# K and V read in 32 KB packets, each written to two partitions through a shape register

## The chip, the cores and the metric

The kernel runs on one core of a Trainium2 chip. The metric is the device time of one execution in microseconds (us). Where a kernel was timed in several rounds, the median is quoted. Before the change the time is 369.1 us.

The page counts 16 DMA engines for the core. A load is issued by one instruction on the queue of SyncE (SP). Each contiguous piece that a load of K or V reads appears in the trace as one *packet*: 64 loads of 128 pieces each, and 8192 packets of 16 KB. The program's tiles lie over 128 partitions of on-chip memory; the loads from DRAM go there. Of the other engines, PE does the matmuls (PEld loads their weights), DVE the transposes and other vector work, ACT and POOL the rest, as the page lists them.

## The reference, cut to what matters

A decode step of attention is mixed with an MLP by a gate. Attention reads the last 2048 keys of a cache, for 8 batches and 16 K/V heads of 128 elements in bf16. K and V of that window are 2 x 8 x 16 x 2048 x 128 x 2 bytes = 134.2 MB of the 154.6 MB that the kernel moves.

```python
k = jnp.repeat(k_cache[:, :, Sk - W:, :], rep, axis=1)      # W = 2048, Sk = 8192, Dh = 128
v = jnp.repeat(v_cache[:, :, Sk - W:, :], rep, axis=1)
scores = jnp.einsum("bhqd,bhkd->bhqk", q, k) * (Dh ** -0.5)
p = _softmax(scores, axis=-1)
o = jnp.einsum("bhqk,bhkd->bhqd", p, v)
...
return g * a + (1 - g) * b        # a: attention @ wo, b: MLP, g: gate
```

Softmax and the sum over keys do not depend on the order of the keys, provided that K and V are ordered alike.

## The kernel before

K and V come in 64 loads of 2 MB, one for four batches of one head ("quad"), into a ring of nine slots. Each load puts 128 pieces of 16 KB (64 keys) into 128 partitions: piece x (of 32) of batch a (of 4) goes to partition 4x + a. The code in question, with cuts:

```python
def run_dma(nc, e, out, in_, shape=None):
    item = 2
    kw = {}
    if shape is not None:
        pst = shape[0]                       # elements in one partition's row
        walk = shape[1]                      # (step, count), slowest first; the last is one contiguous run
        enc = []
        for step, num in reversed(walk[:-1]):
            parts, rest = divmod(step, pst)
            ...
            enc += [parts * 262144 + rest * item, num]
        enc += [0, 1] * (4 - len(enc) // 2)
        kw = dict(dst_dge_shape=enc, bass_dst_dge_shape=tuple(walk))
    return e.add_instruction(mybir.InstDMACopy(..., queue="qSPDynamicHW", mode="Copy",
        ins=e.lower_ap_dma(in_), outs=e.lower_ap_dma(out), **kw))
...
        def src_of(cache, g, q):
            hkv, b0 = 2 * g + q // 2, 4 * (q % 2)
            return cache[b0:b0 + 4, hkv, S0:Sk, :].rearrange("a (x r) d -> x a (r d)", x=32)
...
            # k_unit; v_unit likewise
            d = dma("sp", lambda e: e.dma_start(slot(s), src_of(A_k_cache, g, q)), ...)
            # two DVE transposes of the slot, then QK matmuls from the transposed halves
...
            # wo_chunk: the one load that already goes through the shape register
            src = bass.AP(A_wo.tensor, offset=128 * h0 * D, ap=[[4 * D, 32], [128 * D, WO_CH], [1, 4 * D]])
            d = dma("sp", lambda e: run_dma(nc, e, dst[:, :, 0:D], src, (AST, ((4 * AST, 32), (WOP, WO_CH), (AST, 4), (1, D)))), ...)
```

`AST` is one partition's row, so `(4 * AST, 32)` means "32 times, four partitions further each time". I shall write such a walk as (4 partitions, 32), slowest step first, and leave out the contiguous run at its end. The shape register is the field `dst_dge_shape`. In the program's intent the destination is gone through in that order, while the source is read in the order of its own pattern.

Of the kernel before, what the change touches and what calls it, by code (L numbers as in the profile page):

```python
# [38 lines left out]
class _Plan:  # L39
# [16 lines left out]
    def dma(self, eng, fn, semkey, nbytes, deps=(), name=None, after=(), prio=0):  # L56
        op = _Op(eng, fn, deps, name, self.DMA_ISSUE, after=after, is_dma=True, dma_sem=semkey, nbytes=nbytes, prio=prio)
        op.idx = len(self.all)
        self.all.append(op)
        return op  # L60
# [119 lines left out]
# [4 lines that stand above are left out]
        pst = shape[0]  # L184
        walk = shape[1]
# [3 lines that stand above are left out]
            assert parts == 0 or rest == 0  # L189
# [3 lines that stand above are left out]
    return e.add_instruction(mybir.InstDMACopy(  # L193
        name=nc.get_next_instruction_name(), engine=e.engine, queue="qSPDynamicHW", mode="Copy",
        ins=e.lower_ap_dma(in_), outs=e.lower_ap_dma(out), **kw))


def build_kernel(nc, A_x, A_k_cache, A_v_cache, A_wq, A_wo, B_x, B_w1, B_b1, B_w2, B_b2, gate_w, out):
    B, Sq, D = A_x.shape
    _, Hkv, Sk, Dh = A_k_cache.shape  # L200
    Hq = A_wq.shape[1] // Dh
    F = B_w1.shape[1]
    W = min(4096, max(256, Sk // 4))
# [19 lines left out]
    with ExitStack() as es:  # L223
# [67 lines left out]
        def aoffs(name):  # L291
            return R[name][0] // 2
# [50 lines left out]
        def slot(s):  # L343
            return RAW[:, s * SE:(s + 1) * SE]
# [245 lines left out]
        proj_ops = {}  # L590
        oT_done = {}

        def src_of(cache, g, q):
            hkv, b0 = 2 * g + q // 2, 4 * (q % 2)
            return cache[b0:b0 + 4, hkv, S0:Sk, :].rearrange("a (x r) d -> x a (r d)", x=32)

        def take_slot():
            n = n_slot[0]
# [43 lines left out]
        def k_unit(i):  # L642
            g, q = divmod(i, 4)
            s = take_slot()
            d = dma("sp", lambda e: e.dma_start(slot(s), src_of(A_k_cache, g, q)), "s%d" % s, 4 * W * Dh * 2, deps=slot_free[s], name="dk%d" % i, after=last_dma[-1:])
            last_dma.append(d)
            ub = q
            qrs = []
            for a in range(4):
                def fn(e, a=a):  # L650
                    dst = bass.AP(arena, offset=32 * a * AST + aoffs("qbd") + ub * 512 + 32 * a + 8 * q, ap=[[AST, 32], [128, 4], [1, 8]])
                    src = bass.AP(arena, offset=32 * a * AST + aoffs("q4") + 32 * g + 8 * q, ap=[[AST, 32], [256, 4], [1, 8]])
                    return e.tensor_copy(dst, src)  # L653
                qrs.append(add("pool", fn, deps=[o_q4, o_qz] + [qk_unit.get(i - 4)], name="qr%d_%d" % (i, a), cost=0.2))
            trs = []
            for h in range(2):
                n = 2 * i + h
                kb = n % 2
                deps = [d] + ([qk_half[n - 2]] if n >= 2 else [o_y, o_ssq])
                tr = add("dve", (lambda h=h, kb=kb: lambda e: e.transpose(bass.AP(arena_f, offset=foffs("KT") + kb * 2048, ap=[[AST // 2, 128], [1, 2048]]),  # L660
                                                                         bass.AP(arena_f, offset=foffs("RAW") + s * (SE // 2) + 32 * h, ap=[[AST // 2, 128], [64, 64], [1, 32]])))(),
                         deps=deps, name="tr%d_%d" % (i, h), cost=2.3, after=tr_hist[-1:])
                tr_hist.append(tr)
                trs.append(tr)

                def qk_fn(e, h=h, kb=kb):
                    mm = None
                    if q == 0 and h == 0:
                        e.matmul(ps[:, 0, :], maskL, maskR, start=True, stop=False)  # L669
                        for rc in range(1, 4):  # L670
                            held_matmul(nc, e, ps[:, rc, :], maskL, maskR, start=True, stop=False)
                    for ee in range(2):
                        for rc in range(4):
                            rhs = bass.AP(arena, offset=aoffs("KT") + kb * 4096 + rc * 1024 + ee, ap=[[AST, 128], [2, 512]])
                            args = (ps[:, rc, :], qbd[:, ub, 2 * h + ee, :], rhs)
                            last = q == 3 and h == 1 and ee == 1
                            mm = e.matmul(*args, start=False, stop=last) if rc == 0 else held_matmul(nc, e, *args, stop=last)  # L677
                    return mm
                deps = [tr] + qrs
                if q == 0 and h == 0:  # L680
                    deps += exp_done[g - 1] if g else [o_q4, o_mL, o_mR]
                qk = add("pe", qk_fn, deps=deps, name="qk%d_%d" % (i, h), cost=1.95 + (0.9 if q == 0 and h == 0 else 0), after=qk_half[-1:])
                qk_half.append(qk)
            qk_unit[i] = qk
            slot_free[s] = trs
            if q == 3:
                softmax(g)

        def v_unit(i):
            g, q = divmod(i, 4)  # L690
            s = take_slot()
            item = 2 * g + q // 2
            d = dma("sp", lambda e: e.dma_start(slot(s), src_of(A_v_cache, g, q)), "s%d" % s, 4 * W * Dh * 2, deps=slot_free[s], name="dv%d" % i, after=last_dma[-1:])
            last_dma.append(d)

            def pv_fn(e):
                mm = None
                for t in range(16):
                    c = 32 * (t % 4)
                    mm = e.matmul(ps[c:c + 32, BK_OS[i % 2], :], PT[:, g % 2, 512 * q + 32 * t:512 * q + 32 * t + 32], slot(s)[:, 512 * t:512 * t + 512],  # L700
                                  start=(t < 4), stop=(t >= 12), skip_group_check=True, tile_position=(0, c))
                return mm
            deps = [d] + pt_done[g] + ([u_ev[i - 2]] if i >= 2 else [o_qT, o_u])
            prev = add("pe", pv_fn, deps=deps, name="pv%d" % i, cost=1.5, after=pv_hist[-1:])
            pv_hist.append(prev)
            slot_free[s] = [prev]
            if q == 3:
                pv_last[g] = prev
            u_ev[i] = add("act", lambda e: e.activation(out=EV[:, i % 2, :], in_=ps[:, BK_OS[i % 2], :], func=ACTF.Copy),  # L709
                          deps=[prev] + ([u_sum[i - 2]] if i >= 2 else []), name="uev%d" % i, cost=0.8, prio=3)  # L710

            def us_fn(e):
                mm = None
                for r in range(4):
                    mm = e.matmul(ps[:, BK_S, OC + 16 * (item % 2) + 8 * (q % 2):OC + 16 * (item % 2) + 8 * (q % 2) + 8], EV[:, i % 2, 128 * r:128 * r + 128], i32[:, 8 * r:8 * r + 8],  # L715
                                  start=(r == 0), stop=(r == 3), skip_group_check=True)
                return mm
            u_sum[i] = add("pe", us_fn, deps=[u_ev[i]] + o_i32 + b6_r[-2:], after=b6_w[-1:], name="us%d" % i, cost=1.0, prio=3)
            b6_w.append(u_sum[i])
            if q % 2 == 1:  # L720
                hl = q // 2
                prev = u_sum[i]
                osrc = ps[:, BK_S, OC + 16 * (item % 2):OC + 16 * (item % 2) + 16]
                if item < Hkv - 1:
                    ev = add("act", lambda e: e.activation(out=o32[:, item % 2, :], in_=osrc, func=ACTF.Copy), deps=[prev] + ([oT_done[item - 2]] if item >= 2 else []), name="oev%d" % item, cost=0.25, prio=3)  # L725
                    o_item_ev[item] = ev
                    b6_r.append(ev)
                    eng, src_, deps = "pool", o32[:, item % 2, :], [ev, rg_done[g]]
                else:
                    eng, src_, deps = "dve", osrc, [prev, rg_done[g]]  # L730

                def om_fn(e):
                    return e.tensor_tensor(out=oT[:, item, :, :].rearrange("p h b -> p b h"), in0=src_.rearrange("p (b h) -> p b h", h=2),  # L733
                                           in1=rg[:, g % 2, 16 * hl:16 * hl + 16].rearrange("p (b h) -> p b h", h=2), op=ALU.mult)
                oT_done[item] = add(eng, om_fn, deps=deps, name="oT%d" % item, cost=0.25, prio=9)
# [121 lines left out]
```

## Time and profile before

| what | value |
|---|---|
| time | 369.1 us |
| DMA: K and V packets | 8192 of 16 KB, 611 ns most often, 612 in the mean |
| DMA rate, 45 to 330 us | 430 GB/s, all 16 engines busy |
| DVE, PE busy | 57%, 69% of the span |

The page of the kernel before, its parts on DMA (part 2: busy share of the 16 engines in tenths and GB/s in 40 slices; part 3: the queue's share of 16 engines' time) and on the chain of work that ended last:

```profile
span 367.5 us, 4111 instructions
...
DMA  8999999999999999999999999999999999999994
GB/s 345 428 408 428 428 427 433 432 426 432 435 430 432 422 427 430 432 439 431 426 430 428 422 438 427 430 426 428 433 430 430 428 431 426 433 428 432 418 424 191
DMA packets 11851, 154.59 MB, mean 421 GB/s; under 512 B 1292, under 2 KB 1332, under 8 KB 3000
...
q1 hardware_dynamic: 11776, 154.29, 98.6%
...
DMA 74%; DVE 12%; PE 11%; SPq 1%; ACT 1%; issue 1%; DVEq 0%; ACTq 0%
```

All 16 engines are busy from the first slice to the last but one, and three quarters of the chain are DMA. The kernel is as long as its bytes take. The windows view (busy time of each engine in a stretch, then granted clock, DMA share, GB/s) for the K/V stage of the kernel before says the same:

```profile
core 0: us, PE busy (x) PEld busy (x) DVE busy (x) ACT busy (x) POOL busy (x), PEclk, DMA share, GB/s
...
45.00:330.00 285.00, 203.33 (x1213) 52.45 (x845) 188.66 (x202) 37.92 (x96) 25.72 (x123) 0.86 1.01 430
```

Is the queue kept full? Part 6 of the page (KB of a load, median us from issue to landing), and the waits of SP's queue:

```profile
arena<-in_A_k_cache_dram SPq DMA_DIRECT2D x32, 2048.0 KB, 35.8
arena<-in_A_v_cache_dram SPq DMA_DIRECT2D x32, 2048.0 KB, 36.7
```

```profile
engine line waited for: us in total, times, longest us
SPq L153 <- DVE arena L660: 180.7, 31, 11.8
```

A load of 2 MB takes 4.9 us at 430 GB/s and lands 36 us after its issue: about seven loads stand in the queue. SP waits a lot for DVE to free a slot (L660 is the transpose of K), but ahead of time, so the wait costs nothing.

One line of the page has *under 512 B 1292*. In the packet records these are packets of 4 B. What they are for, the profile does not say.

Last, the lengths of packets on SP's queue, from the trace's packet records (not a view of the profile, so a table of mine; most common length):

| packet | length |
|---|---|
| 4608 B (wo through the register, parts of w1 and w2) | 178 ns |
| 16 KB (K, V) | 611 ns |
| 32 KB (wq) | 1213 ns |
| 36 KB (w1) | 1364 ns |

From 16 KB to 32 KB the length grows by 602 ns, which is 27.2 GB/s for an engine, and leaves 9 ns for each packet as such.

### The profile page before, as it was taken

To read this page: it belongs to the slowest core of one execution; us is meant where nothing else is said; L and a number is where in the kernel's file an instruction comes from. 1 tells how busy PE (TensorE), PEld (TensorE's weight loads), DVE (VectorE), ACT (ScalarE), POOL (GpSimd) and SP (SyncE) were. 2 spreads that over 40 slices of the span, in tenths; PEclk is the share of its full clock that TensorE was granted. 3 is DMA by queue.
4 is the path that set the end of the run, shared out by engine and by line. 5 is a ranking of instruction groups with operands and counts; after the bars stand their busy time and mean duration, and the time that the engine had idled before them with its cause. 6 is when DMAs were issued, how large, how long until landed. Compare 5 with 4: busy or idle time off the path is not lost.

```text
span 367.5 us, 4111 instructions
## 1 busy us (share of the span) xinstructions
PE 254.8 (69%) x1815; PEld 87.3 (24%) x1429; DVE 210.1 (57%) x253; ACT 47.8 (13%) x117; POOL 37.6 (10%) x163
## 2 busy tenths in 40 slices
PE   0349982895598398673986397765966396865995
PEld 0339200131123032010321032111311031214552
DVE  0704699797667754459654764478544864473000
ACT  1010002100300310003000300003100300003200
POOL 7020010011012001000101001010101000000000
PEclk9999998799689879887898879696988789795559
DMA  8999999999999999999999999999999999999994
GB/s 345 428 408 428 428 427 433 432 426 432 435 430 432 422 427 430 432 439 431 426 430 428 422 438 427 430 426 428 433 430 430 428 431 426 433 428 432 418 424 191
DMA packets 11851, 154.59 MB, mean 421 GB/s; under 512 B 1292, under 2 KB 1332, under 8 KB 3000
## 3 DMA queue, kind: packets, MB, share of 16 engines
q1 hardware_dynamic: 11776, 154.29, 98.6%
q8 instruction: 13, 0.21, 0.2%
q10 hardware_dynamic: 56, 0.03, 0.1%
q14 instruction: 6, 0.05, 0.0%
HBM read 154.31 MB, written 0.01 MB: 420 GB/s over the span
## 4 chain that ended last, share of the span: by engine, by line
DMA 74%; DVE 12%; PE 11%; SPq 1%; ACT 1%; issue 1%; DVEq 0%; ACTq 0%
DMA arena<-in_A_k_cache_dram 50%; DMA arena<-in_B_w_dram 15%; DMA arena<-in_A_v_cache_dram 9%; DVE arena L660 9%; PE ps L173 5%; PE ps L516 2%; PE ps L677 1%; DVE arena L605 1%; PE ps L700 1%; SPq L765 1%; ACT arena L619 1%; DVE arena L624 1%; PE ps L518 1%; PE ps L715 1%; DVE arena L614 0%
## 5 line engine op out<-in xcount | busy, mean ns | idle before, releaser
L660 DVE STREAM_TRANSPOSE arena<-arena 128x2048 f32<-128x2048 f32 x64 | 145.2, 2297 | 78.9 <-DMA arena<-in_A_k_cache_dram 71.5
L173 PE MATMUL ps<-arena 128*128 128x512 bf16 x401 | 134.4, 445 | 15.3 <-DVE arena L660 9.8
L677 PE MATMUL ps<-arena 128*128 128x512 bf16 x115 | 51.8, 450 | 16.7 <-DVE arena L660 16.6
L709 ACT ACTIVATE arena<-ps 128x512 f32<-128x512 f32 x32 | 19.1, 598 | 196.7 <-PE ps L700 196.7
L677 PEld LDWEIGHTS ps<-arena 128*128 128x128 bf16 x128 | 14.6, 114 | 125.8 <-issue 66.8
L715 PE MATMUL ps<-arena 128*128 128x8 f32 x256 | 36.9, 275 | 8.7 <-ACT arena L709 7.7
L653 POOL COPY arena<-arena 32x32 bf16<-32x32 bf16 x128 | 26.0, 203 | 159.2 <-PE ps L173 144.6
L715 PEld LDWEIGHTS ps<-arena 128*128 128x128 f32 x256 | 35.6, 217 | 22.4 <-ACT arena L709 16.4
L700 PE MATMUL ps<-arena 128*32 128x512 bf16 x512 | 36.7, 413 | 6.0 <-DMA arena<-in_A_v_cache_dram 6.0
L669 PE MATMUL ps<-arena 128*128 128x512 bf16 x6 | 3.5, 585 | 37.8 <-DVE arena L624 37.8
L605 DVE TENSOR_REDUCE arena<-ps 128x1 f32<-128x2048 f32 x8 | 18.3, 2282 | 15.5 <-PE ps L173 15.5
L619 ACT ACTIVATE arena<-ps,arena 128x512 bf16<-128x512 f32 x32 | 21.6, 686 | 41.4 <-DVE arena L614 41.4
L700 PEld LDWEIGHTS ps<-arena 128*32 128x32 bf16 x512 | 11.3, 100 | 39.8 <-issue 24.1
L624 DVE STREAM_TRANSPOSE arena<-arena 128x512 bf16<-128x512 bf16 x32 | 19.8, 674 | 0.9 <-ACT arena L619 0.9
L733 POOL TENSOR_TENSOR arena<-arena 128x16 bf16<-128x16 f32 x15 | 4.0, 267 | 142.3 <-ACT arena L725 142.3
L516 PE MATMUL ps<-arena 128*128 128x8 bf16 x144 | 10.9, 201 | 4.5 <-DMA arena<-in_B_w_dram 4.5
L559 PE MATMUL ps<-arena 128*8 128x288 bf16 (+1 forms) x140 | 11.6, 315 | 1.9 <-DMA arena<-in_B_w_dram 1.7
L516 PEld LDWEIGHTS ps<-arena 128*128 128x128 bf16 x144 | 10.8, 159 | 5.0 <-DMA arena<-in_B_w_dram 5.0
L669 PEld LDWEIGHTS ps<-arena 128*128 128x128 bf16 x8 | 0.9, 107 | 45.1 <-DVE arena L624 45.1
L733 DVE TENSOR_TENSOR arena<-ps,arena 128x16 bf16<-128x16 f32 x1 | 0.2, 229 | 19.4 <-PE ps L715 19.4
L438 PE MATMUL ps<-arena 8*128 8x8 bf16 x8 | 0.5, 168 | 13.5 <-DVE arena L411 9.8
L631 DVE RECIPROCAL arena<-ps 128x32 f32<-128x32 f32 x8 | 2.9, 358 | 10.5 <-PE ps L629 10.5
(83 smaller groups left out, 95.6 us busy)
## 6 DMA issues: line engine op xcount, KB each, us to landing
arena<-in_A_k_cache_dram SPq DMA_DIRECT2D x32, 2048.0 KB, 35.8
arena<-in_A_v_cache_dram SPq DMA_DIRECT2D x32, 2048.0 KB, 36.7
arena<-in_B_w_dram SPq DMA_DIRECT2D x1, 4608.0 KB, 24.3
arena<-in_A_wq_dram SPq DMA_DIRECT2D x1, 4096.0 KB, 13.1
arena<-in_B_w_dram SPq DMA_DIRECT2D x3, 1296.0 KB, 33.9
arena<-in_B_w_dram SPq DMA_DIRECT2D x2, 576.0 KB, 28.7
arena<-in_A_wq_dram SPq DMA_DIRECT2D x1, 512.0 KB, 3.7
arena<-in_B_w_dram SPq DMA_DIRECT2D x1, 432.0 KB, 30.4
```

Source lines behind the costliest of these rows:

```text
L173: return e.add_instruction(mybir.InstMatmult(name=nc.get_next_instruction_name(), engine=mybir.EngineType.PE, ins=[e.lower_ap(rhs), e.lowe ...
L516: ins = e.matmul(out_, lhsT, yT[:, kt, :], start=(kt == 0), stop=False)
L559: ins = e.matmul(ps[32 * j:32 * j + 8, BK_ACC, 0:JN], lhsT, rhs[:, JN * j:JN * j + JN], start=False, stop=True, skip_group_check=True, til ...
L605: mx = add("dve", lambda e: e.tensor_reduce(out=k(MX), in_=ps[:, 0:4, :].rearrange("p a n -> p (a n)"), axis=AXL.X, op=ALU.max), deps=[qk_ ...
L619: return e.activation(out=Pm[:, 512 * c:512 * c + 512], in_=ps[:, c, :], func=ACTF.Exp, bias=k(NB), scale=SCALE, accum_out=k(SUM + c))
L624: pts.append(add("dve", (lambda c=c: lambda e: e.transpose(bass.AP(arena, offset=aoffs("PT") + 2048 * (g % 2) + 128 * c, ap=[[AST, 128], [ ...
L653: return e.tensor_copy(dst, src)
L660: tr = add("dve", (lambda h=h, kb=kb: lambda e: e.transpose(bass.AP(arena_f, offset=foffs("KT") + kb * 2048, ap=[[AST // 2, 128], [1, 2048]]),
L677: mm = e.matmul(*args, start=False, stop=last) if rc == 0 else held_matmul(nc, e, *args, stop=last)
L700: mm = e.matmul(ps[c:c + 32, BK_OS[i % 2], :], PT[:, g % 2, 512 * q + 32 * t:512 * q + 32 * t + 32], slot(s)[:, 512 * t:512 * t + 512], st ...
L709: u_ev[i] = add("act", lambda e: e.activation(out=EV[:, i % 2, :], in_=ps[:, BK_OS[i % 2], :], func=ACTF.Copy), deps=[prev] + ([u_sum[i - ...
L715: mm = e.matmul(ps[:, BK_S, OC + 16 * (item % 2) + 8 * (q % 2):OC + 16 * (item % 2) + 8 * (q % 2) + 8], EV[:, i % 2, 128 * r:128 * r + 128 ...
```

## The change

The intent is to spare half of those 9 ns. A read of 32 KB fetches two neighbouring pieces at once, and the shape register is to split the write over two partitions. Both halves go to partitions p and p + 32, and the 16 blocks of 32 KB begin at partitions 64 x hi + 4 x lo, one block for each of 16 engines.

```diff
-        def src_of(cache, g, q):
+        def load_quad(e, cache, g, q, s):
             hkv, b0 = 2 * g + q // 2, 4 * (q % 2)
-            return cache[b0:b0 + 4, hkv, S0:Sk, :].rearrange("a (x r) d -> x a (r d)", x=32)
+            blk = 2 * 64 * Dh
+            src = bass.AP(cache.tensor, offset=((b0 * Hkv + hkv) * Sk + S0) * Dh, ap=[[blk, 16], [Hkv * Sk * Dh, 4], [1, blk]])
+            dst = bass.AP(arena, offset=aoffs("RAW") + s * SE, ap=[[AST, 128], [SE, 1], [1, SE]])
+            return run_dma(nc, e, dst, src, (AST, ((64 * AST, 2), (4 * AST, 8), (AST, 4), (32 * AST, 2), (1, 64 * Dh))))
...
-            d = dma("sp", lambda e: e.dma_start(slot(s), src_of(A_k_cache, g, q)), ...)
+            d = dma("sp", lambda e: load_quad(e, A_k_cache, g, q, s), ...)
...
-            d = dma("sp", lambda e: e.dma_start(slot(s), src_of(A_v_cache, g, q)), ...)
+            d = dma("sp", lambda e: load_quad(e, A_v_cache, g, q, s), ...)
```

More of the change, by code (lines that the diff above doesn't have):

```diff
@@ L644, in k_unit @@
             s = take_slot()
-            d = dma("sp", lambda e: e.dma_start(slot(s), src_of(A_k_cache, g, q)), "s%d" % s, 4 * W * Dh * 2, deps=slot_free[s], name="dk%d" % i, after=last_dma[-1:])
+            d = dma("sp", lambda e: load_quad(e, A_k_cache, g, q, s), "s%d" % s, 4 * W * Dh * 2, deps=slot_free[s], name="dk%d" % i, after=last_dma[-1:])
             last_dma.append(d)
@@ L692, in v_unit @@
             item = 2 * g + q // 2
-            d = dma("sp", lambda e: e.dma_start(slot(s), src_of(A_v_cache, g, q)), "s%d" % s, 4 * W * Dh * 2, deps=slot_free[s], name="dv%d" % i, after=last_dma[-1:])
+            d = dma("sp", lambda e: load_quad(e, A_v_cache, g, q, s), "s%d" % s, 4 * W * Dh * 2, deps=slot_free[s], name="dv%d" % i, after=last_dma[-1:])
             last_dma.append(d)
```

## The prediction

k is the number of engines that a K/V load uses. The case k = 2 stands as an assumption. No term of the sum is cut: 64 loads of 38.8 us are 2480 us, and with 57 us for the rest it came to 2537 us (2535 on record).

> **What bounds it now.** DMA. The page's queue table has the SP queue's packets at 98.6% of the 16 engines' span; the DMA view gives 430 GB/s from 45 to 330 us; the chain of waits is 74% DMA. The other engines have room (DVE 57%, PE 69% busy), and the queue runs about seven loads ahead (36 us from issue to landing for a 2 MB load that takes 4.9 us), so neither compute nor issue sets the pace. K and V are 134.2 of 154.6 MB.
>
> **What a packet costs.** In the trace's packet records a K or V packet (16 KB) takes 611 ns, a 32 KB packet of wq 1213, a 36 KB packet of w1 1364: one line, 27.2 GB/s for each engine plus 9 ns for each packet. The wo packets, read as 4608 B and already split over four partitions through a shape register, take 178 ns like unsplit ones of that size (185 in the mean): the split write costs little.
>
> **What the change does.** 8192 packets of 16 KB become 4096 of 32 KB. PE, DVE, ACT and POOL keep their instructions and order; K and V are permuted alike. Both halves of a packet go to partitions p and p+32[...].
>
> *If all 16 engines are used:* each spares 256 x 9 ns = 2.3 us (1.5 us if the small overlap of packets, 100.6% of the time between 45 and 330 us, is taken off), all on the critical path: 367 us, "same".
>
> **The catch: how many engines.** [...] The instruction names a destination of 128 partitions, but the walk in the shape register has (64 partitions, 2) slowest. wo's walk has 32 there, the old K/V patterns 32 and 128: 16 engines for both. If the register's pattern counts, k = 2; no run of this case shows that yet. Then each K/V load is 32 packets on each of two engines, 32 x 1.21 = 38.8 us in place of 4.9. 64 x 38.8 = 2480 us, and the rest of the span (369 - 512 x 0.61 = 57 us) stays: 2537 us. All compute hides.
>
> I find k = 2 likelier (6 in 10): [...]. But the author clearly meant 16 chunks, one for each engine, and the range has to hold both outcomes.
>
> **Predicted: 2535 us, range 364 to 2620** (two modes, about 367 and about 2535; little between). Faster by over 2%: 0.02; within 2%: 0.36; slower by over 2%: 0.62.
>
> **What would show it.** Either way about 7755 packets in place of 11851, the 32 KB ones near 1213 ns. With k = 2: DMA share near 0.13 in the K/V stage, some 54 GB/s, landing of a K/V load near 270 us, the chain nearly all K and V DMA. With k = 16: DMA share near 1.0, 432 to 433 GB/s, landing still 35 us.
>
> **What would make it wrong.** k taken from the instruction's 128; a lone engine not running at 27.2 GB/s when 14 others idle; [...].

## The result, and the profile after

The changed kernel takes 2556.0 us (2555.6 to 2557.0, 6 runs) against 369.1 us, a ratio of 6.925 (95% interval 6.916 to 6.934). Ratios in this document are the mean time of one kernel's fast runs over the mean of the other's fast runs of the same rounds, so not quite the ratio of the medians quoted.

The page of the changed kernel, the same lines as before:

```profile
span 2554.5 us, 4175 instructions
...
DMA  4111111111111111111111111111111111111114
GB/s 191 54 54 55 54 54 54 54 54 54 54 54 68 54 54 54 54 54 54 54 54 69 53 55 54 54 54 54 54 53 55 69 54 54 54 54 54 54 69 112
DMA packets 6859, 154.58 MB, mean 61 GB/s; under 512 B 396, under 2 KB 436, under 8 KB 2104
...
q1 hardware_dynamic: 6784, 154.29, 14.7%
...
another core or an unknown queue 86%; PE 6%; DVE 5%; DMA 2%; SPq 1%; issue 0%; ACTq 0%; POOL 0%; DVEq 0%; ACT 0%
...
arena<-in_A_k_cache_dram SPq DMA_DIRECT2D x32, 16.0 KB
arena<-in_A_v_cache_dram SPq DMA_DIRECT2D x32, 16.0 KB
```

Three readings. First, the DMA engines are busy for a tenth of the time and move 54 GB/s, which is twice 27.2: two engines' worth. Second, 396 packets under 512 B are 268 + 64 x 2, where the 1292 before are 268 + 64 x 16 (the 268 belong to everything else): by this count two engines for each K/V load, not 16. Third, the profile no longer names K and V in the chain (86% is "an unknown queue") and gives no landing time for them. (Nor are its 16.0 KB the size of a load: the bytes in total, 154.58 MB, are as before.) So the landing time that I predicted, 270 us, cannot be checked here; who waited for K and V is still named in the waits, first of the kernel before, then of the changed one:

```profile
engine line waited for: us in total, times, longest us
...
DVE arena L660 <- DMA arena<-in_A_k_cache_dram: 71.5, 17, 10.4
```

```profile
engine line waited for: us in total, times, longest us
...
DVE arena L663 <- DMA arena<-in_A_k_cache_dram: 2016.0, 32, 73.0
...
PE ps L703 <- DMA arena<-in_A_v_cache_dram: 1100.7, 32, 75.6
```

Before, DVE waited 71.5 us in all for K. Now its transposes (the same ones, three lines further down in the changed file) wait 2016 us, up to 73 us at a time. The windows view of the changed kernel:

```profile
core 0: us, PE busy (x) PEld busy (x) DVE busy (x) ACT busy (x) POOL busy (x), PEclk, DMA share, GB/s
...
100.00:1000.00 900.00, 114.50 (x466) 25.81 (x297) 83.58 (x85) 14.36 (x37) 12.43 (x60) 0.55 0.13 55
```

A share of 0.13 is 2 of 16. The granted clock has fallen to 0.55, but PE is busy for an eighth of this window: it is not what the kernel waits for. In the packet records the 4096 packets of K and V have a median of 1214 ns and a mean of 1223 ns. A packet is as fast as it was for wq. There are only two engines to work them off: between 89 and 689 us two packets of K and V are under way at 2982 of 3001 moments taken at equal distances.

### The profile page after: what moved, and what is told of

It is laid out like the page before. It is cut to its first block, busy times and chain, and to the rows that moved or that the text cites. A ratio compares the mean times of both kernels' runs of the same rounds, so it can differ in the third digit from the quotient of the medians.

```text
span 2554.5 us, 4175 instructions
## 1 busy us (share of the span) xinstructions
PE 346.4 (14%) x1815; PEld 111.6 (4%) x1429; DVE 209.8 (8%) x253; ACT 47.3 (2%) x117; POOL 37.5 (1%) x163
## 2 busy tenths in 40 slices
DMA packets 6859, 154.58 MB, mean 61 GB/s; under 512 B 396, under 2 KB 436, under 8 KB 2104
## 4 chain that ended last, share of the span: by engine, by line
another core or an unknown queue 86%; PE 6%; DVE 5%; DMA 2%; SPq 1%; issue 0%; ACTq 0%; POOL 0%; DVEq 0%; ACT 0%
PE ps L173 3%; DVE arena L663 3%; SPq L768 1%; PE ps L680 1%; DMA arena<-in_B_w_dram 1%; PE ps L703 1%; DVE arena L608 1%; DMA arena<-in_B_b_dram 0%; DVE arena L627 0%; PE ps L718 0%; PE ps L482 0%; DVE arena L617 0%; DVE arena L611 0%; DVE arena L634 0%
## 5 line engine op out<-in xcount | busy, mean ns | idle before, releaser
L703 PE MATMUL ps<-arena 128*32 128x512 bf16 x512 | 60.7, 627 | 1100.7 <-DMA arena<-in_A_v_cache_dram 1100.7
L173 PE MATMUL ps<-arena 128*128 128x512 bf16 x401 | 171.7, 550 | 181.4 <-DVE arena L663 177.8
L680 PE MATMUL ps<-arena 128*128 128x512 bf16 x115 | 65.0, 565 | 650.2 <-DVE arena L663 650.2
L718 PE MATMUL ps<-arena 128*128 128x8 f32 x256 | 53.3, 342 | 8.7 <-ACT arena L712 7.7
L718 PEld LDWEIGHTS ps<-arena 128*128 128x128 f32 x256 | 52.5, 305 | 30.8 <-ACT arena L712 18.4
L672 PE MATMUL ps<-arena 128*128 128x512 bf16 x6 | 3.6, 605 | 242.6 <-DVE arena L663 202.5
L516 PE MATMUL ps<-arena 128*128 128x8 bf16 x144 | 10.9, 201 | 4.0 <-DMA arena<-in_B_w_dram 4.0
L518 PE MATMUL ps<-arena 128*128 128x8 bf16 x36 | 7.2, 201 | 0.0
```

Of the source, the lines that this page charges most:

```text
L173: return e.add_instruction(mybir.InstMatmult(name=nc.get_next_instruction_name(), engine=mybir.EngineType.PE, ins=[e.lower_ap(rhs), e.lowe ...
L516: ins = e.matmul(out_, lhsT, yT[:, kt, :], start=(kt == 0), stop=False)
L680: mm = e.matmul(*args, start=False, stop=last) if rc == 0 else held_matmul(nc, e, *args, stop=last)
L703: mm = e.matmul(ps[c:c + 32, BK_OS[i % 2], :], PT[:, g % 2, 512 * q + 32 * t:512 * q + 32 * t + 32], slot(s)[:, 512 * t:512 * t + 512], st ...
L718: mm = e.matmul(ps[:, BK_S, OC + 16 * (item % 2) + 8 * (q % 2):OC + 16 * (item % 2) + 8 * (q % 2) + 8], EV[:, i % 2, 128 * r:128 * r + 128 ...
```

## The experiments

What is known so far is that two engines carry K and V. Why is not. Theory A, in the form that the measured two engines and the 2 in the walk suggest: the smaller of the two slowest counts, of source and destination, sets the number of engines, up to 16, and for a shape register the destination's is the slowest count of the *walk*, here 2, whatever the instruction says of 128 partitions. Rival B: large packets, or packets split over two partitions by a four-step walk, go to few engines. Rival C: the register path is slow in itself. The first four runs tell these apart. Each changes only `load_quad` of the changed kernel.

A caution that holds for all of them: "correct" says little of where keys land. Two runs below put batches on wrong partitions on purpose and still passed the comparison with the reference. That the permuted order is right rests on the code.

### e1: exchange the two outermost steps

```diff
-            ... ((64 * AST, 2), (4 * AST, 8), (AST, 4), (32 * AST, 2), (1, 64 * Dh))
+            ... ((4 * AST, 8), (64 * AST, 2), (AST, 4), (32 * AST, 2), (1, 64 * Dh))
```

> The changed kernel with the two outermost steps of the walk exchanged: (4 partitions, 8) slowest, then (64 partitions, 2). Packets of 32 KB, halves 32 partitions apart, as in the changed kernel. Theory A [...]: 8 engines; 268 + 64 x 8 = 780 packets under 512 B; 64 x 8 packets x 1.213 + 57 = about 678 us; DMA share near 0.5 in the K/V stage. Rival B (the slowness is of large packets split over two partitions by a four-step walk): 2556 us and 396 small packets, as for the changed kernel.

Measured: 689.7 us. The page's DMA lines of e1:

```profile
DMA packets 7243, 154.58 MB, mean 225 GB/s; under 512 B 780, under 2 KB 820, under 8 KB 2488
...
q1 hardware_dynamic: 7168, 154.29, 54.1%
```

780 small packets and a share of 0.52 of the 16 engines between 45 and 330 us: eight engines, as theory A said. The packets are the same 32 KB, split over the same pairs of partitions, by a walk of the same four steps. Only the order of two steps was exchanged, which also permutes the blocks once more. The median packet is 1214 ns. Rival B falls in its strong form.

### e2 and e3: the old packets through the register

e2 goes back to 16 KB, one partition for each packet, and to the old placement, but with a slowest count of 2:

```diff
-            blk = 2 * 64 * Dh
-            src = ... ap=[[blk, 16], [Hkv * Sk * Dh, 4], [1, blk]])
+            blk = 64 * Dh
+            src = ... ap=[[blk, 32], [Hkv * Sk * Dh, 4], [1, blk]])
-            ... ((64 * AST, 2), (4 * AST, 8), (AST, 4), (32 * AST, 2), (1, 64 * Dh))
+            ... ((64 * AST, 2), (4 * AST, 16), (AST, 4), (1, 64 * Dh))
```

> The packets (16 KB, one partition each) and the placement of the kernel before, but written through the register with the walk (64 partitions, 2), (4 partitions, 16), (1 partition, 4). Theory A: slowest count 2, so 2 engines: 396 small packets, 64 x 64 packets x 0.611 + 57 = about 2560 us. Rival B (packet size and split are the cause): 369 us, 1292 small packets.

e3 is e2 with the first two steps of the walk joined into one:

```diff
-            ... ((64 * AST, 2), (4 * AST, 16), (AST, 4), (1, 64 * Dh))
+            ... ((4 * AST, 32), (AST, 4), (1, 64 * Dh))
```

> As the run before it, but with the walk (4 partitions, 32), (1 partition, 4): the register alone, at the old packets and placement. Theory A: 16 engines, 369 us within 0.3%, 1292 small packets, packets of 611 ns. A rival C, by which the register path itself is slow to issue or generate: clearly over 369 us, the DMA share falling below 0.99.

Measured: e2 2562.6 us. The DMA lines of its page:

```profile
DMA packets 10955, 154.58 MB, mean 60 GB/s; under 512 B 396, under 2 KB 436, under 8 KB 2104
...
q1 hardware_dynamic: 10880, 154.29, 14.6%
```

e3 369.3 us (4 runs), ratio 1.0003 (95% interval 0.9989 to 1.0018). Its page:

```profile
DMA packets 11851, 154.59 MB, mean 421 GB/s; under 512 B 1292, under 2 KB 1332, under 8 KB 3000
...
q1 hardware_dynamic: 11776, 154.29, 98.7%
```

These two kernels read the same bytes in the same order, in the same packets, and write them to the same partitions. (64 partitions, 2), (4, 16) and (4 partitions, 32) go through the same partitions in the same order. The one written with an outermost 2 uses two engines (396 small packets), the other 16 (1292). That it also has one step more is not what counts: e1 and the changed kernel have four steps each and use eight engines and two, and e8 below has three, like e2, and uses 16. With 16 KB packets and single partitions e2 is as slow as the changed kernel, so rival B is gone; with the register e3 is as fast as before, so rival C is gone. The cause of the result is the outermost count of 2. How the counts lead to the number of engines in general is not settled by this; e10 below goes against theory A in its general form.

### e4: 32 KB packets on 16 engines

Could the change be had with its intent? By theory A it needs a slowest count of 16, and so the 16 blocks at equal distances, for example 8 partitions, with the halves 4 apart:

```diff
-            ... ((64 * AST, 2), (4 * AST, 8), (AST, 4), (32 * AST, 2), (1, 64 * Dh))
+            ... ((8 * AST, 16), (AST, 4), (4 * AST, 2), (1, 64 * Dh))
```

> 32 KB packets, halves 4 partitions apart: walk (8 partitions, 16), (1, 4), (4, 2). Theory A: 16 engines, 1292 small packets. If packets then keep 1213 ns, 366.8 to 367.6 us (256 x 9 ns less per engine, or 1.5 us with the overlap taken off). [...] Rival B: about 2556 us.

Measured: 571.0 us median of 4 runs (558.6 to 587.1), ratio 1.547 (1.534 to 1.560). These runs spread by 5%, two of them slow (575.1 and 587.1). The two fast, 558.6 and 566.8, are 1.52 times the kernel before. The profile is that of the 558.6 us run. The DMA line of e4's page, and its windows view in the K/V stage:

```profile
DMA packets 7755, 154.59 MB, mean 278 GB/s; under 512 B 1292, under 2 KB 1332, under 8 KB 3000
```

```profile
core 0: us, PE busy (x) PEld busy (x) DVE busy (x) ACT busy (x) POOL busy (x), PEclk, DMA share, GB/s
45.00:330.00 285.00, 149.41 (x754) 34.20 (x495) 124.36 (x136) 24.93 (x64) 18.33 (x88) 0.76 1.00 267
```

All 16 engines are used (1292) and always busy (1.00), but they move 267 GB/s. A packet now takes 1943 ns in the mean in place of 1214. So here it is not the number of engines but the speed of each. Theory P: engines slow each other, and which partitions they write at the same time decides it. Rival Q: a packet split over partitions 4 apart is slow. Which engines write which partitions, and which partitions would clash, no trace shows.

### e5 to e8: who writes which partitions, and loads without a register

e5, a slowest count of 4 in the walk, with the halves 4 partitions apart as in e4:

```diff
-            ... ((64 * AST, 2), (4 * AST, 8), (AST, 4), (32 * AST, 2), (1, 64 * Dh))
+            ... ((8 * AST, 4), (32 * AST, 4), (AST, 4), (4 * AST, 2), (1, 64 * Dh))
```

> 32 KB packets; walk (8 partitions, 4), (32, 4), (1, 4), (4, 2). Theory A: slowest counts 16 and 4, so 4 engines, 268 + 64 x 4 = 524 small packets. [...] Theory P [...] expects packets of 1214 ns [...]: 64 x 16 x 1.22 + 57 = about 1306 us.

Measured: 1313.4 us, 524 packets under 512 B, median packet 1214 ns. Four engines, as theory A says. Moreover the packets are split over partitions 4 apart, as in e4, and are not slow (a median of 1214 ns, against e4's mean of 1943). Rival Q falls.

e6, the same packets with the batch as the slowest step of both sides:

```diff
-            src = ... ap=[[blk, 16], [Hkv * Sk * Dh, 4], [1, blk]])
+            src = ... ap=[[Hkv * Sk * Dh, 4], [blk, 16], [1, blk]])
-            ... ((64 * AST, 2), (4 * AST, 8), (AST, 4), (32 * AST, 2), (1, 64 * Dh))
+            ... ((AST, 4), (64 * AST, 2), (4 * AST, 8), (32 * AST, 2), (1, 64 * Dh))
```

> The changed kernel's packets and partitions, but the batch is the slowest step on both sides: source (batch, 4), (block, 16); walk (1 partition, 4), (64, 2), (4, 8), (32, 2). Theory A: 4 engines, 524 small packets. [...] Rival Q ([...] e4 was slow because a packet split over partitions 4 apart is slow): about 1306 us [...].

This run failed: the runtime reported that the program had completed with an error (code 1004), and there is no profile. It was not repeated, so whether it fails each time, and why, is open. e10 below bears on it.

e7, no shape register at all; the source has its slowest count at 4:

```diff
-            blk = 2 * 64 * Dh
-            src = ... ap=[[blk, 16], [Hkv * Sk * Dh, 4], [1, blk]])
+            blk = 64 * Dh
+            src = ... ap=[[Hkv * Sk * Dh, 4], [blk, 32], [1, blk]])
-            return run_dma(nc, e, dst, src, (AST, (...)))
+            return run_dma(nc, e, dst, src)
```

> No shape register: plain destination of 128 partitions, 16 KB packets, source with the batch slowest: (batch, 4), (block, 32). The result is wrong on purpose (batches land on other partitions). Theory A, of any pattern: slowest counts 4 and 128, so 4 engines, 524 small packets, 64 x 32 x 0.611 + 57 = about 1310 us if packets keep 611 ns; [...]. If only a shape register limits the engines (rival D): 1292 small packets.

Measured: 1349.7 us, 524 packets under 512 B: four engines without any register. Rival D falls: a plain load whose source has a slowest count of 4 got four engines too. The windows view of e7:

```profile
core 0: us, PE busy (x) PEld busy (x) DVE busy (x) ACT busy (x) POOL busy (x), PEclk, DMA share, GB/s
32.00:50.00 18.00, 6.37 (x107) 6.28 (x105) 0.00 (x0) 0.00 (x0) 0.00 (x0) 1.00 0.25 59
50.00:70.00 20.00, 4.31 (x14) 0.48 (x4) 6.47 (x7) 0.89 (x2) 0.00 (x0) 1.00 0.25 69
70.00:90.00 20.00, 1.38 (x7) 0.10 (x1) 2.05 (x3) 0.00 (x0) 0.82 (x4) 0.63 0.25 96
90.00:110.00 20.00, 6.01 (x16) 0.54 (x4) 5.07 (x3) 0.00 (x0) 0.82 (x4) 0.59 0.25 108
```

Four engines are busy throughout (0.25), but start at 59 GB/s, about half of four times 27.2, and reach 108 in the window from 90 us on. What changes in those 60 us is not shown: no view tells which engine writes or reads what. e7 also reads in another order than the kernel before, and no run separates that from the writes.

e8, the old packets on the old partitions, with a slowest step of 8 partitions and count 16 in the walk:

```diff
-            blk = 2 * 64 * Dh
-            src = ... ap=[[blk, 16], [Hkv * Sk * Dh, 4], [1, blk]])
+            blk = 64 * Dh
+            src = ... ap=[[blk, 32], [Hkv * Sk * Dh, 4], [1, blk]])
-            ... ((64 * AST, 2), (4 * AST, 8), (AST, 4), (32 * AST, 2), (1, 64 * Dh))
+            ... ((8 * AST, 16), (4 * AST, 2), (AST, 4), (1, 64 * Dh))
```

> Packets (16 KB, one partition) and placement of the kernel before, walk (8 partitions, 16), (4, 2), (1, 4). Theory A: 16 engines, 1292 small packets. [...] Theory P: packets clearly over 611 ns[...]. Rival Q [...]: 611 ns and 369 us.

Measured: 678.3 us. e8's page, and the windows view of e3 and then of e8:

```profile
DMA packets 11851, 154.59 MB, mean 228 GB/s; under 512 B 1292, under 2 KB 1332, under 8 KB 3000
```

```profile
core 0: us, PE busy (x) PEld busy (x) DVE busy (x) ACT busy (x) POOL busy (x), PEclk, DMA share, GB/s
45.00:330.00 285.00, 213.25 (x1240) 53.90 (x849) 189.08 (x197) 37.87 (x96) 26.16 (x125) 0.84 1.01 430
```

```profile
45.00:330.00 285.00, 133.35 (x598) 30.20 (x385) 106.82 (x117) 20.28 (x52) 15.37 (x74) 0.71 1.01 222
```

e3 and e8 are a close pair: the same packets, the same partition for each byte, 16 engines in both. What can differ is which engine carries which packet, and when. e3 moves 430 GB/s with packets of 611 ns, e8 222 GB/s with a mean of 1195 ns, longer than e3's mean of 612 ns by a factor of 1.95. Theory P expected packets clearly over 611 ns; its ranges, 800 to 1200 ns and 480 to 680 us, held.

But an engine that carries other packets also reads elsewhere. If each engine takes an equal run of the source, which the traces do not show, the 16 engines of e4, e8 and e9 read 32 KB apart; in e3 they may not. No run changes the reads alone, so the rival that it is the reads which get in each other's way stands. Two things speak against it. wq's 128 packets come from pieces 32 KB apart too, so its engines read at multiples of 32 KB from each other, and the most common length is 1213 ns (mean 1249 in the kernel before), far from double. And e9, next, reads the source in the same pattern as e8 and yet begins much slower (132 against 213 GB/s). So theory P is the better account of e4 and e8, but it is not shown.

### e9 and e10: how far each theory goes

e9 is e8 with another walk, (1 partition, 16), then (16, 8):

```diff
-            ... ((8 * AST, 16), (4 * AST, 2), (AST, 4), (1, 64 * Dh))
+            ... ((AST, 16), (16 * AST, 8), (1, 64 * Dh))
```

> 16 KB packets, 16 engines; the source is read as in e8, only the walk differs: (1 partition, 16), (16, 8), [...] The result is wrong on purpose (batches land on other partitions). Theory A: 1292 small packets. [...] Rival R (any assignment but the natural one costs the same factor): about 678 us again.

Measured: 776.6 us. The windows view of e9, at its start and later:

```profile
core 0: us, PE busy (x) PEld busy (x) DVE busy (x) ACT busy (x) POOL busy (x), PEclk, DMA share, GB/s
35.00:50.00 15.00, 8.41 (x139) 8.29 (x137) 1.97 (x1) 0.00 (x0) 0.00 (x0) 1.00 1.00 132
...
100.00:200.00 100.00, 31.89 (x144) 6.46 (x99) 35.49 (x46) 7.55 (x20) 3.50 (x17) 0.62 1.01 170
...
500.00:700.00 200.00, 89.13 (x421) 22.37 (x301) 56.19 (x57) 12.47 (x31) 7.00 (x33) 0.67 1.01 213
```

The direction is that of theory P, which had e9 slower than e8: 132 GB/s at first, clearly below e8's 213 GB/s in its first window (32 to 50 us). The size is not: the author's figure was about 1310 us. The rate rises during the run, to 213 GB/s between 500 and 700 us; why, as in e7, is not shown. Rival R (e8's factor for any assignment of packets to engines other than that of the kernel before) does not fit the early rate.

e10, in place of e6, the batch slowest on both sides with 16 KB packets:

```diff
-            blk = 2 * 64 * Dh
-            src = ... ap=[[blk, 16], [Hkv * Sk * Dh, 4], [1, blk]])
+            blk = 64 * Dh
+            src = ... ap=[[Hkv * Sk * Dh, 4], [blk, 32], [1, blk]])
-            ... ((64 * AST, 2), (4 * AST, 8), (AST, 4), (32 * AST, 2), (1, 64 * Dh))
+            ... ((AST, 4), (4 * AST, 32), (1, 64 * Dh))
```

> In place of e6, which failed: batch slowest on both sides, 16 KB packets, placement of the kernel before; walk (1 partition, 4), (4, 32). Theory A: 4 engines, 524 small packets. [...] as e7's rate suggests (59 GB/s at 32 to 50 us, 108 from 90 us on): slow at first, then packets of 611 ns and 108 GB/s, about 1320 to 1500 us.

Measured: 369.0 us. The DMA lines of e10's page:

```profile
DMA packets 11851, 154.59 MB, mean 421 GB/s; under 512 B 1292, under 2 KB 1332, under 8 KB 3000
...
q1 hardware_dynamic: 11776, 154.29, 98.6%
```

A miss, and a useful one. Both slowest counts are 4, yet 16 engines are used (1292), at 612 ns in the mean, undisturbed. So "the slowest count decides" is not the whole rule. The compiler had not rearranged anything: e10 was built again, and its instruction still has a slowest count of 4 in the source and in the register. What makes the difference is not shown. In e10 the counts of source and walk, 4 and 32, match step by step; in e2 (two engines), 32 and 4 against 2, 16 and 4, they do not, and e7 (four engines), with the same source as e10, has no register. e6, which failed, also had the batch slowest, but no matching second step.

### The runs side by side

Engines are read from the packets under 512 B. The packet lengths come from the packet records of the profiled run, which for e4 is the one of 558.6 us.

| run | walk (partitions, count), slowest first | packet | engines, from small packets | K/V packet, mean | time |
|---|---|---|---|---|---|
| before | none | 16 KB | 16 (1292) | 612 ns | 369.1 us |
| e3 | (4, 32), (1, 4) | 16 KB | 16 (1292) | 612 ns | 369.3 us |
| e10 | (1, 4), (4, 32) | 16 KB | 16 (1292) | 612 ns | 369.0 us |
| e4 | (8, 16), (1, 4), (4, 2) | 32 KB | 16 (1292) | 1943 ns | 571.0 us |
| e8 | (8, 16), (4, 2), (1, 4) | 16 KB | 16 (1292) | 1195 ns | 678.3 us |
| e1 | (4, 8), (64, 2), (1, 4), (32, 2) | 32 KB | 8 (780) | 1238 ns | 689.7 us |
| e9 | (1, 16), (16, 8) | 16 KB | 16 (1292) | 1391 ns | 776.6 us |
| e5 | (8, 4), (32, 4), (1, 4), (4, 2) | 32 KB | 4 (524) | 1230 ns | 1313.4 us |
| e7 | none; source slowest 4 | 16 KB | 4 (524) | 633 ns | 1349.7 us |
| after | (64, 2), (4, 8), (1, 4), (32, 2) | 32 KB | 2 (396) | 1223 ns | 2556.0 us |
| e2 | (64, 2), (4, 16), (1, 4) | 16 KB | 2 (396) | 615 ns | 2562.6 us |

Except for e8, e9 and e4, where packets are disturbed, the time is, within 1%, the packets of one engine times their length, plus 57 us for the rest. No version with 32 KB packets beat the kernel before. The change wanted three things at once: 32 KB packets, 16 engines, and its own choice of partitions. Its blocks begin at 64 x hi + 4 x lo, which is no row of 16 equal steps. So a walk that begins with the blocks has an outermost count of 2 or 8, and got as many engines (396 small packets after the change, 780 in e1). With 16 equal steps (e4) packets take 1943 ns in the mean, by theory P because of the partitions that engines write at the same time; that is not shown. Whether the change can be had with the batch outermost, as e10 has it for 16 KB, is open: the one such version that ran (e6) failed. And the prize was small: 256 packets less for each engine, 9 ns each, 2.3 us at most.

## Why the prediction was right or wrong

- *The bound.* Right. DMA was the limit before, and with fewer engines it is the only one: the share of 0.13 and the 2016 us that DVE waits for K show it.
- *k = 2.* Right, and held at 6 in 10 only. Whether the register's walk counts, or the 128 partitions that the instruction names, no trace before could tell, since the loads of the kernel before whose engines can be counted, K and V (1292 small packets), used 16. e1, e2 and e3 show that the walk counts (8, 2 and 16 engines). e10 (4 outermost, 16 engines) shows that the outermost count is not all that matters.
- *The time.* 2537 us from the sum against 2556. The term that was mis-sized is the length of a packet: I put in 1.21 us; the 4096 packets took 1.223 us in the mean (median 1.214, with 49 over 1.33). 2048 x 1.223 = 2505, and 2505 + 57 = 2562 us, near the 2556 measured.
- *The range.* It held, but as it had to hold two modes, from 364 to 2620 us, that says little. The weight on "slower", 0.62, was the real statement.
- *About 7755 packets.* Wrong: 6859. The difference is 896 = 64 x 14: I halved the data packets but forgot the packets of 4 B, of which a K/V load now has two in place of 16, one for each engine that takes part. That forgotten term became the best indicator.
- *54 GB/s, share 0.13, packets near 1213 ns.* Right.
- *Landing near 270 us, and a chain of K and V DMA.* Not to be checked: the profile gives no landing for these loads and calls 86% of the chain an unknown queue.
- *The split write costs little.* Right: packets split over two partitions have a median of 1214 ns in e1, e5 and in the changed kernel. That the register costs nothing was not forecast in words, only assumed in the sum; e3, at 1.0003 of before, shows it.
- *Two risks, of writes and of reads that get in each other's way.* The changed kernel met neither (its packets have a median of 1214 ns). e4 (571 us, mean packet 1943 ns) and e8 (678 us, 1195 ns) lost time in such a way; that the writes are the reason is theory P, better supported than the reads but not shown.

## What to carry to other kernels

When a load's access pattern is rewritten, count the engines that it will use before weighing anything else: a factored outermost step, (64, 2), (4, 16) in place of (4, 32), cost a factor of seven for the same bytes in the same places. Look at the run for it: e10, with an outermost count of 4, used all 16. The count of packets under 512 B shows the number of engines at a glance; so does the rate divided by one engine's 27.2 GB/s, but only where packets keep their usual length (e4 and e8, with 16 engines, would be taken for ten and eight). And when a rewritten walk has its 16 engines but not the rate of the natural 128-partition load (e4 and e8: 267 and 222 GB/s), suspect which engine carries which partition: e8 differs from e3 in the walk alone. That this is the reason is not shown.
